# Batch 1's attention output as plain float32 products, the weight decode spread over steps, expert 0 loaded in stage 3, and later block gathers

## The chip, the cores and the metric

One core of one Trainium2 chip. The metric is the device time of the kernel in microseconds (us), the median of several executions. The engines are TensorE (PE, its weight loads PEld), VectorE (DVE), ScalarE (ACT), GpSimd (POOL) and SyncE (SP, which issues most of the DMAs). The instructions of one engine run in order.

## The reference

Three parts follow each other; all data are float32:

```python
# attention: 4 batches, 8 heads, 576 positions, 64 wide
decay = cum[:, :, :, None] - cum[:, :, None, :]      # cum = cumsum(log f)
attn  = softmax(where(causal, -1e9, q @ k.T / 8 + decay))
x     = (attn @ v) regrouped to 2304 tokens x 512
# MoE1, dense: 512 -> 1536 -> 512
x = (silu(x @ w_gate) * (x @ w_val)) @ w_out
# MoE2, top-1 of 8 experts, 512 -> 1024 -> 512
out[t] = gate_w[t] * eom[t, e] * (relu(x[t] @ w1[e]) @ w2[e]),  e = argmax(x[t] @ w_gate)
```

## The kernel before

**Number form.** Most products run in float32r. An operand is split into a high part (a copy to float32r, by ACT) and a low part (the difference, by DVE or POOL), and a product is the sum of two or three float32r products.

**Attention** (class Attention, L41 to L290) handles one head at a time. `load` (L96) brings q, k and v in; `split` (L105) makes high and low parts, those of v at L126 (ACT) and L127 (POOL); `qk` (L130) makes scores (L152, L153), their maximum (L156, DVE) and the exponential (L164, ACT). `tr` (L168) transposes the exponentials in four groups into PSUM and writes a high part `ath` (ACT, L191) and a low part `atl` (DVE, L192). `av` (L195) multiplies them by v: ten matmuls at L207 for positions 64 to 575 and two at L216 for the first 64. The stationary operand holds high v in 64 columns and low v in the other 64, so half of the result is moved by ACT (L211, L217) and added by DVE (L212, L218). `xout` (L238) normalises and splits the head pair into `xth` and `xtl`, the input of MoE1.

**MoE1** (class MoE1, L305 to L435) has five stages of 12 units, one stage for each token chunk of 512 or 384 (the last is reordered). A unit is `gv` (24 matmuls, L378, then tanh and two DVE operations) and, one unit later, `out` (12 matmuls, L403). Both are generators that yield after every three matmuls, 12 steps for a unit; at each step the loop in `tile_kernel` also runs a share of the attention of the next batch (`MIX`, L448). So heads 0 to 7 run alone, heads 8 to 15 (batch 1) during stage 0, and batches 2 and 3 during stages 1 and 2.

**Decode.** The MoE1 weights lie in memory as 64-bit words (`mw`). In stage 0 each of the 36 pieces is loaded (L328, one of two `raw` buffers), squared (L332, ACT), worked on by four DVE operations (L333 to L336), and split into the weight tile (L338, ACT; L339, POOL). A finished tile is also written back to DRAM (L341, L343, by SP), from which later stages fetch it (`fetch`, L345, by POOL's queue). `ready` (L353) emits the decode of the unit three ahead in one go, two pieces when a `gv` ends and one when an `out` ends; six pieces are emitted at the start of stage 0.

**MoE2** (class MoE2, from L660). Per expert, token rows are gathered (L709, POOL), transposed (L693), split (L695, L696); four units of `g1` (24 matmuls of 304 columns, L728) and `g2` (24, L743) follow. `load_expert` (L647) brings a quarter of one expert: two loads of 512 KB (L652), each split by ACT (L654) and DVE (L655) into two tiles of the weight pools. The quarter u=0 of expert 0 is loaded near the end of MoE1 (L1019, through the two buffers of the pool `raw2`), the quarters 1 to 3 after MoE1 (L1059). Tokens beyond the 304 slots of an expert go to a block: `block_a` (L780, called at expert 4, quarter 3) gathers rows and weights (`b_y`, `b_g`, `b_r`, all by L709), `block_b` (L833, called at expert 6) multiplies them.

**Order.** A scheduler orders each engine's instructions by priority, which is the order of the program text, and by its own estimate of readiness. `tc.issue_after(x)` keeps what it encloses behind x.

Of the kernel before, what the change touches and what calls it, by code (L numbers as in the profile page):

```python
# [40 lines left out]
class Attention:  # L41
    def __init__(self, tc, ctx, cst, io, xth, xtl, ps_s, ps_t, ps_x):
# [14 lines left out]
        fix = pool("at_fix", 1, side="right")  # L57
        self.e0 = [fix.tile([128, 128], F32, name=f"e0_{i}") for i in range(2)]
# [4 lines left out]
        for t in self.e0 + [t.bitcast(F32) for t in self.hl]:  # L63
            nc.gpsimd.memset(t, 0.0)
# [31 lines left out]
    def load(self, h):  # L96
        nc = self.nc
        qk = self.raw.tile([128, 2, S], F32, name="qkd")
        for o in (0, 64):
            nc.sync.dma_start(out=qk[o:o + 64], in_=self.io["qk"][h])  # L100
        v = self.raw.tile([128, 5, D], F32, name="vraw")
        nc.sync.dma_start(out=v, in_=self.io["vL"][h])
        self.R[h] = qk, v

    def split(self, h):  # L105
# [17 lines left out]
        self.K[h] = (a, b, kh, kl)  # L123
        vs = self.stk.tile([128, 5, 2, D], F32R, name="vs")
# [43 lines left out]
    def tr(self, h, g):  # L168
# [15 lines left out]
        else:  # L184
# [3 lines left out]
            nc.tensor.transpose(tp[:, 256:384], E[h, 0], ident)  # L188
        th = self.ap[g].tile([128, n], F32R, name=f"ath{g}")
# [5 lines left out]
    def av(self, h):  # L195
# [6 lines left out]
        z, c = self.Z[h // 2]  # L202
        ax = self.ps_x()
        terms = [(0, 0, 0, 512, 0), (1, 1, 0, 512, 0), (2, 2, 0, 384, 128), (4, 2, 384, 128, 384), (3, 3, 0, 256, 256)]
        for t, (j, g, s, n, d0) in enumerate(terms):
            for i in range(2):
                nc.tensor.matmul(ax[:, d0:d0 + n], st[:, j], self.T[h, g][i][:, s:s + n],  # L207
                                 start=t == 0 and i == 0, stop=t == 4 and i == 1)
            if t == 1:
                yield 900  # L210
        nc.scalar.activation(c[m:m + 64, 64:], ax[o:o + 64], ACTF.Copy)  # L211
        nc.vector.tensor_add(z[m:m + 64, 64:], ax[m:m + 64], c[m:m + 64, 64:])  # L212
        yield 600
        ay = self.ps_t()
        for i in range(2):
            nc.tensor.matmul(ay[:, :64], st[:, 0], self.T[h, 3][i][:, 256:320], start=i == 0, stop=i == 1)  # L216
        nc.scalar.activation(c[m:m + 64, :64], ay[o:o + 64, :64], ACTF.Copy)  # L217
        nc.vector.tensor_add(z[m:m + 64, :64], ay[m:m + 64, :64], c[m:m + 64, :64])  # L218
        for g in range(4):
            del self.T[h, g]  # L220
        yield 220
# [83 lines left out]
class MoE1:  # L305
    def __init__(self, tc, ctx, io, xth, xtl):
# [8 lines left out]
        self.dec = None  # L315

    def decode(self, ft, kind):
# [14 lines left out]
        nc.scalar.activation(s, hv.bitcast(F32), ACTF.Square)  # L332
        nc.vector.tensor_scalar(t, hv, 0x07ffffff, 3, op0=ALU.bitwise_and, op1=ALU.logical_shift_left)  # L333
        nc.vector.scalar_tensor_tensor(t, hv, -0x40000000, t, op0=ALU.bitwise_and, op1=ALU.bitwise_or)  # L334
        nc.vector.scalar_tensor_tensor(t, lv, 29, t, op0=ALU.logical_shift_right, op1=ALU.bitwise_or)  # L335
        nc.vector.scalar_tensor_tensor(s, s, 2.0 ** -30, t.bitcast(F32), op0=ALU.is_ge, op1=ALU.mult)  # L336
        s3 = s.rearrange("p (a b) -> p a b", a=4)
# [14 lines left out]

    def ready(self, i, out):  # L353
# [4 lines left out]
        elif out:  # L358
            self.decode(i, 2)
        else:  # L360
            self.decode(i, 0)
            self.decode(i, 1)
# [49 lines left out]
    def steps(self, done):  # L412
# [7 lines left out]
        for i in range(len(us) + LAG):  # L420
            if i < len(us):
                u = us[i]
                yield u
                yield from self.gv(u)
# [3 lines left out]
            if i >= LAG:  # L428
                u = us[i - LAG]
                yield from self.out(u)  # L430
# [16 lines left out]
APB = (1, 2, 1, 1)  # L447
MIX = 0.46  # L448
# [211 lines left out]
class MoE2:  # L660
# [47 lines left out]
    def gather(self, dst, src, ix):  # L708
        self.nc.gpsimd.indirect_dma_start(out=dst, out_offset=None, in_=src[:, :],  # L709
# [227 lines left out]
def tile_kernel(tc, io, out, dbg=None):  # L937
    nc = tc.nc
    with ExitStack() as ctx:
# [19 lines left out]
        with ExitStack() as cx:  # L959
# [5 lines left out]
            for i in range(3):  # L965
                m1.decode(0, i)
# [17 lines left out]
        slots, w00 = None, None  # L984
# [10 lines left out]
        for st in m1.steps(done):  # L995
            if isinstance(st, tuple):
                if st[0] != stage:
# [4 lines left out]
                    if stage == 0:  # L1002
                        for i in range(6):
                            m1.decode(1 + i // 3, i % 3)
# [5 lines left out]
                    if stage == 3:  # L1010
# [6 lines left out]
                        wts.pools = [pool(ctx, "wA", 6, side="right")]  # L1017
                        raw = pool(cm, "raw2", 2)
                if st[0] == 4 and st[2] == 4 * NF + 5:  # L1019
# [107 lines left out]
```

## Time and profile before

| | us |
|---|---|
| median of 3 runs (lowest, highest) | 1080.6 (1076.13, 1085.01) |
| the profiled execution | 1079.55 |
| its span in the trace | 1077.8 |
| heads 0 to 7 alone | 0 to 94 |
| stage 0 of MoE1, with batch 1's heads and 33 decodes | 94 to 296 |
| stages 1, 2, then 3 and 4 of MoE1 | 296 to 468, to 617, to 775 |
| routing tail | 775 to 796 |
| MoE2 | 796 to 1066 |

The trace is that of one execution. Times count from the start of the span. The busy time of an engine in a stretch says how much work it had; what a stage is bound by is read from the waits and from the chain of work that ended last. The end of a matmul is modelled, so its pace is read from the starts of long uninterrupted rows.

### The profile page before, as it was taken

The numbers are of one execution on the slowest core, as the hardware profiler recorded it, in microseconds if no ns is written. First come the engines' busy times: TensorE is split into PE (matmuls) and PEld (weight loads), VectorE is DVE, ScalarE is ACT, GpSimd is POOL, SyncE is SP. The second block draws the span as 40 slices with busy tenths as digits, with TensorE's granted clock in tenths as the row PEclk, the third lists the DMA queues.
The fourth block names the chain that finished last, engine by engine and source line by source line (L and its number), as shares of the span: only waits on it lengthen the run. The fifth ranks groups of instructions, "written<-read, shape, count | busy, mean of one in ns | idle before, by whom it ended". The sixth has DMA issues, their size and how long they took to land.

```text
span 1077.8 us, 15687 instructions
## 1 busy us (share of the span) xinstructions
PE 974.9 (90%) x5488; PEld 837.4 (78%) x5488; DVE 583.1 (54%) x1293; ACT 523.5 (49%) x1083; POOL 428.8 (40%) x463
## 2 busy tenths in 40 slices
PE   3788788888899999999999999999987999999894
PEld 2666566665667787777777899999876999999794
DVE  6779998888654644344444431152274555452820
ACT  5697555555465545465454431221233544543721
POOL 4556664455443443533442323223154633332111
PEclk9798999999989999999999999999978999999998
DMA  7646565657966565765444577367458656552500
GB/s 203 171 115 186 191 225 198 221 190 234 301 159 190 164 173 158 191 203 167 145 147 130 192 244 240 106 212 241 169 177 304 192 173 189 168 173 76 170 28 26
DMA packets 69956, 192.49 MB, mean 179 GB/s; under 512 B 9317, under 2 KB 29815, under 8 KB 62580
## 3 DMA queue, kind: packets, MB, share of 16 engines
q1 hardware_dynamic: 51411, 106.51, 33.1%
q0 software_dynamic: 18464, 84.96, 24.6%
q8 instruction: 44, 0.72, 0.3%
q14 instruction: 37, 0.29, 0.1%
HBM read 158.10 MB, written 29.14 MB: 174 GB/s over the span
## 4 chain that ended last, share of the span: by engine, by line
PE 50%; issue 15%; DVE 6%; POOL 5%; DMA 4%; ACT 2%; POOLq 0%; SPq 0%; DVEq 0%; ACTq 0%
PE ps_g L378 21%; PE ps_y L403 11%; PE ps_t L207 3%; PE m_psy L743 3%; PE m_psg L728 2%; POOL out L769 2%; PE ps_s L152 1%; DMA raw<-mw 1%; PE ps_s L153 1%; DMA raw<-w 1%; DVE dt L335 1%; DMA qb<-qkh 1%; POOL yg L709 1%; DVE dt L334 1%; PE ps_t L179 1%
## 5 line engine op out<-in xcount | busy, mean ns | idle before, releaser
L728 PE MATMUL m_psg<-ygh,w 128*128 128x304 f32 x512 | 117.3, 310 | 6.9 <-DVE h2l L731 4.2
L743 PE MATMUL m_psy<-h2h,w 128*128 128x304 f32 x512 | 115.7, 308 | 0.1
L192 DVE TENSOR_TENSOR atl<-ps_t,ath 128x512 fp32r<-128x512 f32 (+1 forms) x128 | 81.3, 636 | 51.6 <-ACT ath L191 51.4
L164 ACT ACTIVATE e<-e,mx 64x64 f32<-64x64 f32 (+4 forms) x160 | 88.9, 557 | 35.7 <-DVE mx L156 34.4
L655 DVE TENSOR_TENSOR w<-raw,w 128x1024 fp32r<-128x1024 f32 x64 | 77.2, 1229 | 50.2 <-ACT w L654 27.6
L191 ACT ACTIVATE ath<-ps_t 128x512 fp32r<-128x512 f32 (+1 forms) x128 | 70.3, 554 | 61.5 <-PE ps_t L183 18.0
L389 POOL TENSOR_TENSOR hl<-hs,hh 128x512 fp32r<-128x512 f32 (+1 forms) x60 | 70.9, 1181 | 60.7 <-ACT hh L388 60.6
L383 DVE SCALAR_TENSOR_TENSOR hs<-hs,ps_g 128x512 f32<-128x512 f32 (+1 forms) x60 | 37.9, 631 | 103.9 <-ACT hs L382 103.8
L728 PEld LDWEIGHTS m_psg<-ygh,w 128*128 128x128 f32 x512 | 87.1, 192 | 7.9 <-DVE h2l L731 4.4
L156 DVE CUSTOM_DVE_ANT_0 e<-ps_s,mask 64x64 f32<-64x64 f32 (+4 forms) x160 | 66.6, 424 | 48.9 <-PE ps_s L153 42.9
L654 ACT ACTIVATE w<-raw 128x1024 fp32r<-128x1024 f32 x64 | 67.4, 1058 | 46.2 <-DMA raw<-w 16.7
L743 PEld LDWEIGHTS m_psy<-h2h,w 128*128 128x128 f32 x512 | 86.7, 190 | 0.9 <-issue 0.5
L769 POOL DMA_INDIRECT out<-o,sl_idx x24 | 31.5, 1313 | 121.1 <-ACT o L765 120.2
L152 PE MATMUL ps_s<-qkh 128*128 128x288 f32 (+3 forms) x192 | 62.8, 338 | 18.4 <-DVE qkh L121 9.2
L743 PE MATMUL m_psy<-h2l,w 128*128 128x304 f32 x256 | 78.4, 306 | 1.2 <-issue 1.2
L728 PE MATMUL m_psg<-ygl,w 128*128 128x304 f32 x256 | 78.1, 305 | 0.0
L382 ACT ACTIVATE hs<-ps_g 128x512 f32<-128x512 f32 (+1 forms) x60 | 33.1, 551 | 87.8 <-PE ps_g L378 73.5
L731 DVE SCALAR_TENSOR_TENSOR h2l<-m_psg,h2h 128x304 fp32r<-128x304 f32 x64 | 30.2, 472 | 67.7 <-ACT h2h L730 66.4
L153 PE MATMUL ps_s<-kl,qb 68*128 68x288 f32 (+3 forms) x192 | 57.8, 317 | 8.3 <-DMA qb<-qkh 8.2
L121 POOL TENSOR_TENSOR qkh<-qkd,qkh 64x576 fp32r<-64x576 f32 x31 | 45.6, 1472 | 46.3 <-ACT qkh L118 41.6
L152 PEld LDWEIGHTS ps_s<-qkh 128*128 128x128 f32 (+1 forms) x192 | 36.1, 191 | 35.8 <-DVE mx L156 20.6
L388 ACT ACTIVATE hh<-hs 128x512 fp32r<-128x512 f32 (+1 forms) x60 | 35.1, 585 | 56.6 <-DVE hs L385 56.5
(934 smaller groups left out, 2756.3 us busy)
## 6 DMA issues: line engine op xcount, KB each, us to landing
raw<-w SPq DMA_DIRECT2D x64, 512.0 KB
qkd<-qk SPq DMA_DIRECT2D x64, 288.0 KB
raw<-mw SPq DMA_DIRECT2D x36, 512.0 KB
vraw<-vL SPq DMA_DIRECT2D x32, 160.0 KB
qb<-qkh SPq DMA_DIRECT2D x32, 144.0 KB
yd<-yr SPq DMA_DIRECT2D x18, 256.0 KB
wdg<-wg__284 SPq DMA_DIRECT2D x1, 1024.0 KB
wdg<-wg__1288 SPq DMA_DIRECT2D x1, 1024.0 KB
```

The costliest lines, as they stand in the source:

```text
L152: nc.tensor.matmul(ps[:m, :n], a[:, q0:w], kh[:, lo:hi], start=True, stop=False)
L153: nc.tensor.matmul(ps[:m, :n], b[:, q0:w], kl[:, lo:hi], start=False, stop=True)
L164: nc.scalar.activation(e[:m, :w], e[:m, :w], ACTF.Exp, bias=prev[:m], scale=-1.0, accum_out=rs[:m, c:c + 1])
L191: nc.scalar.activation(th, tp[:, :n], ACTF.Copy)
L192: nc.vector.tensor_sub(tl, tp[:, :n], th.bitcast(F32))
L378: nc.tensor.matmul(p, w[:, a, 4 * m + k], x, start=k == 0 and j == 0, stop=k == 3 and j == 2)
L389: nc.gpsimd.tensor_sub(hl, t, hh.bitcast(F32))
L403: nc.tensor.matmul(self.Y[c][d], w[:, a, d], x, start=first and j == 0, stop=last and j == 2)
L654: nc.scalar.activation(hi, r, ACTF.Copy)
L655: nc.vector.tensor_sub(lo, r, hi.bitcast(F32))
L728: nc.tensor.matmul(ps[:, :C], w[:, k, fs], x[:, k], start=(k == 0 and c == 0), stop=(k == 3 and c == 2))
L743: nc.tensor.matmul(self.P[e][d][:, :C], w[:, f, ds], h[:, f], start=(u == 0 and f == 0 and c == 0), stop=(u == 3 and f == 1 and c == 2))
```

## The change

The change has four parts, and a constant for each is set anew.

1. **Decode one operation at a time.** `decode` becomes a generator that yields after each of its first five operations. `ready` only queues pieces (`queue`); each step of MoE1 pulls one operation, or two if more than three pieces are queued; `flush` completes a piece before the unit that uses it.
2. **Batch 1 in plain float32** (`WIDE`, heads 8 to 15). The transposed exponentials are copied once, as float32 (groups 0 and 2 by ACT, 1 and 3 by DVE), the products of `av` are five and one instead of ten and two, with plain v in a stationary operand whose other 64 columns are zero, and ACT alone writes z. v is loaded straight into that operand (`load_v`, after the products of the head two before), so it needs no split. The shares of attention (`MIX`) and buffers of one group (`APB`) change with it.
3. **Expert 0 loaded early.** Three quarters are loaded around the end of stage 2, into a pool opened there; only the fourth is loaded after MoE1.
4. **Block gathers later.** `block_a` is placed behind the last gather emitted before it.

```diff
@@ class Attention
+        self.vst = [fix.tile([128, 5, 2, D], F32, name=f"vst{i}") for i in range(2)]
...
+    def load_v(self, h):
+        if WIDE[0] <= h < WIDE[1]:
+            self.nc.sync.dma_start(out=self.vst[h % 2][:, :, h % 2], in_=self.io["vL"][h])
+            self.V[h] = self.vst[h % 2]
...
+        if WIDE[0] <= h < WIDE[1]:
+            t = self.ap[g].tile([128, n], F32R, name=f"at{'hl'[h % 2]}{g}").bitcast(F32)
+            if g % 2:
+                nc.vector.tensor_copy(t, tp[:, :n])
+            else:
+                nc.scalar.activation(t, tp[:, :n], ACTF.Copy)
+            self.T[h, g] = (t,)
+            return
...
-            for i in range(2):
+            for i in range(parts):
...
+        if wide:
+            yield 1000
+            nc.scalar.activation(z[m:m + 64, 64:], ax[m:m + 64], ACTF.Copy)
+        else:
+            nc.scalar.activation(c[m:m + 64, 64:], ax[o:o + 64], ACTF.Copy)
+            nc.vector.tensor_add(z[m:m + 64, 64:], ax[m:m + 64], c[m:m + 64, 64:])
...
+        if h >= WIDE[0]:
+            self.load_v(h + 2)
@@ class MoE1
         nc.scalar.activation(s, hv.bitcast(F32), ACTF.Square)
+        yield
         nc.vector.tensor_scalar(t, hv, 0x07ffffff, 3, op0=ALU.bitwise_and, op1=ALU.logical_shift_left)
+        yield
...
+    def queue(self, ft, kinds):
+        self.dq += [(ft, k, self.decode(ft, k)) for k in kinds]
+
+    def pull(self):
+        if self.dq and next(self.dq[0][2], 0) == 0:
+            self.dq.pop(0)
...
-        elif out:
-            self.decode(i, 2)
         else:
-            self.decode(i, 0)
-            self.decode(i, 1)
+            self.queue(i, (2,) if out else (0, 1))
@@ constants
-APB = (1, 2, 1, 1)
-MIX = 0.46
+APB = (1, 1, 1, 1)
+MIX = (0.62, 0.46, 0.46)
+WIDE = (8, 16)
@@ tile_kernel
-                        wts.pools = [pool(ctx, "wA", 6, side="right")]
+                        wA, wC = pool(ctx, "wA", 6, side="right"), pool(ctx, "wC", 12, side="right")
+                        wts.pools = [wA, wC, wC]
...
-                if st[0] == 4 and st[2] == 4 * NF + 5:
-                    w00 = load_expert(nc, io, wts, raw, 0, 0)
+                if st[0] == 4 and st[2] >= 4 * NF + 3 and st[2] % 2:
+                    w00.append(load_expert(nc, io, wts, raw, 0, len(w00)))
...
+            for _ in range(2 if len(m1.dq) > 3 else 1):
+                m1.pull()
-            while att and ca_ < cm_ * MIX:
+            while att and ca_ < cm_ * MIX[stage]:
...
-                for u in range(1, 4):
+                for u in range(len(w00), 4):
...
-                    blk = m2.block_a(pblk, cur, rt)
+                    with tc.issue_after(m2.pmark.ins):
+                        blk = m2.block_a(pblk, cur, rt)
```

What moves on SP in stage 0, where `vraw` and `vst` are the buffers of v, `raw` those of the decode, `wdg` and `wdo` the write-backs. Before, some units into the stage:

```order
L100 DMA qkd<-qk 64x1152 [waits DMAHW4_49]
L328 DMA raw<-mw 128x1024 [waits DMAHW5_49,DVE_49,Activation_49]
L102 DMA vraw<-vL 128x320 [waits DMAHW6_49,Pool_49]
L114 DMA qb_156<-cd 2x576 [waits DMAHW7_49,PE_49]
L341 DMA wdg_83<-wg__1288 128x2048 [waits DMAHW0_49,Pool_49]
L328 DMA raw<-mw 128x1024 [waits DMAHW1_49,DMAHW3_49,DVE_49,Activation_49]
L343 DMA wdo_84<-wo__1312 128x1024 [waits DMAHW2_49,Pool_49]
```

And now, at the same place:

```order
L101 DMA qkd<-qk 64x1152 [waits DMAHW4_49]
L112 DMA vst_152<-vL 128x5x64 [waits DMAHW5_49,PE_49]
L359 DMA raw<-mw 128x1024 [waits DMAHW1_49,DVE_49,Activation_49]
L377 DMA wdg_85<-wg__1447 128x2048 [waits DMAHW7_49,Pool_49]
L379 DMA wdo_86<-wo__1505 128x1024 [waits DMAHW0_49,Pool_49]
L359 DMA raw<-mw 128x1024 [waits DMAHW2_49,DVE_49]
L359 DMA raw<-mw 128x1024 [waits DMAHW6_49,DVE_49,Activation_49]
```

The load of v now waits for PE (the products of the head two before) and has the next decode's load behind it; before, it waited for POOL.

On SP at the boundary of stages 2 and 3, from the last load of attention on; `raw<-w` are the loads of expert 0 and `yd<-yr` the rows that MoE1 writes for the gathers. Before:

```order
L119 DMA qb_158<-qkh 64x576 [waits DMAHW7_49,Activation_49]
L652 DMA raw<-w 128x4x256 [waits DMAHW3_49,DMAHW2_49,DMAHW5_49,DMAHW1_49,DMAHW6_49,DMAHW0_49,DMAHW7_49,PE_49,Activation_49]
L652 DMA raw<-w 128x2x512
L503 DMA yd<-yr 128x512 [waits Activation_49] x2
L503 DMA yd<-yr 128x512 [waits DMAHW4_49,Activation_49]
```

Now:

```order
L129 DMA qb_160<-qkh 64x576 [waits DMAHW7_49,Activation_49]
L699 DMA raw<-w 128x4x256 [waits DMAHW3_49,DMAHW2_49,DMAHW5_49,DMAHW1_49,DMAHW6_49,DMAHW0_49,DMAHW7_49,PE_49,Activation_49]
L699 DMA raw<-w 128x2x512
L699 DMA raw<-w 128x4x256 [waits DMAHW0_49,DVE_49,Activation_49]
L699 DMA raw<-w 128x2x512 [waits DMAHW1_49,DVE_49]
L699 DMA raw<-w 128x4x256 [waits DMAHW4_49,DMAHW2_49,DVE_49]
L699 DMA raw<-w 128x2x512 [waits DMAHW3_49,DVE_49]
L550 DMA yd<-yr 128x512 [waits Activation_49] x6
```

All six loads stand ahead of the row writes, and the third to sixth wait until ACT and DVE have emptied the two buffers. The conversions stand in ACT's queue between the operations of the units that run there.

On POOL at the start of MoE2, `yg` are gathers of token rows, `b_r` and `b_y` those of the block. Before:

```order
L709 DMA yg<-yd,sl_idx 48x512
L709 DMA b_r_9994<-w,b_wi 128x1024
L709 DMA yg<-yd,sl_idx 128x512 x2
L709 DMA yg<-yd,sl_idx 48x512
L709 DMA b_r_9998<-w,b_wi 128x1024
L709 DMA b_r_10002<-w,b_wi 128x1024
L709 DMA b_r_10006<-w,b_wi 128x1024
L709 DMA yg<-yd,sl_idx 128x512
```

Now:

```order
L756 DMA yg<-yd,sl_idx 48x512
L756 DMA yg<-yd,sl_idx 128x512 x2
L756 DMA yg<-yd,sl_idx 48x512
L756 DMA yg<-yd,sl_idx 128x512 x2
L756 DMA yg<-yd,sl_idx 48x512
L756 DMA gate<-gd,sl_idx 128x1 x2
```

The twelve gathers of `b_r` have left this place; they stand between the output scatters of a middle expert, behind the row gathers of expert 5.

## Rows read from the trace of the kernel before

**Rows 1.** Busy time of each engine in stretches of the span, core 0.

```profile
core 0: us, PE busy (x) PEld busy (x) DVE busy (x) ACT busy (x) POOL busy (x), PEclk, DMA share, GB/s
...
94.00:296.00 202.00, 165.24 (x754) 125.70 (x754) 171.99 (x298) 110.53 (x231) 107.96 (x94) 0.94 0.69 220
...
775.00:834.00 59.00, 44.20 (x251) 38.95 (x250) 33.83 (x100) 24.21 (x40) 25.24 (x24) 0.83 0.73 248
834.00:999.00 165.00, 164.56 (x1197) 162.12 (x1197) 82.50 (x114) 79.34 (x129) 62.76 (x55) 1.00 0.51 159
```

**Rows 2.** Groups of instructions on DVE in stage 0, 94 to 296 us.

```profile
line engine op names shapes xcount | busy us, mean ns | idle before us <-releasers
L335 DVE SCALAR_TENSOR_TENSOR dt<-raw,dt 128x512 int32<-128x512 int32 x33 | 33.8, 1023 | 0.1
L334 DVE SCALAR_TENSOR_TENSOR dt<-raw,dt 128x512 int32<-128x512 int32 x32 | 33.7, 1053 | 0.4
L336 DVE SCALAR_TENSOR_TENSOR ds<-ds,dt 128x512 f32<-128x512 f32 x33 | 27.8, 843 | 0.3
L333 DVE TENSOR_SCALAR dt<-raw 128x512 int32<-128x512 int32 x31 | 25.2, 814 | 3.2 <-DMA raw<-mw 3.2
L192 DVE TENSOR_TENSOR atl<-ps_t,ath 128x512 fp32r<-128x512 f32 (+1 forms) x32 | 20.3, 635 | 9.8 <-ACT ath L191 9.7
...
L212 DVE TENSOR_TENSOR z<-ps_t,c 64x512 f32<-64x512 f32 x7 | 4.8, 683 | 0.1
...
L218 DVE TENSOR_TENSOR z<-ps_t,c 64x64 f32<-64x64 f32 x8 | 1.7, 218 | 1.0 <-ACT c L217 0.9
```

**Rows 3.** SP's waits in stage 0, longest in total first.

```profile
engine line waited for: us in total, times, longest us
SPq L328 <- DVE dt L335: 57.4, 19, 5.1
SPq L341 <- POOL wg__1918 L339: 7.1, 1, 7.1
```

**Rows 4.** The chain that ended last, from 264 to 276 us in stage 0.

```profile
261.57 2.95 DVE dt L335
264.52 0.02 SPq L328
264.55 0.03 issue
264.57 8.35 DMA raw<-mw
272.92 0.02 issue
...
273.59 0.42 ACT ath L191
274.01 0.48 ACT hs L382
274.49 0.53 ACT wg__2737 L338
```

**Rows 5.** Groups on ACT in stage 0, 94 to 296 us.

```profile
L332 ACT ACTIVATE ds<-raw 128x512 f32<-128x512 f32 x32 | 21.4, 668 | 10.6 <-DMA raw<-mw 9.3 <-POOL wg__1325 L339 0.9 <-POOL wg__1563 L339 0.2
```

**Rows 6.** The chain from 648 us on, in stage 3, PE uninterrupted (384 columns).

```profile
648.49 4.16 PE ps_g L378 x24
652.65 2.08 PE ps_y L403 x12
```

**Rows 7.** The chain at the start of MoE2, 796 to 840 us.

```profile
799.55 5.05 DMA raw<-w
...
817.84 7.46 DMA raw<-w
...
828.41 0.42 PE m_pst L693 x4
...
833.84 3.34 PE m_psg L728 x24
```

**Rows 8.** Groups on PE at the start of MoE2, 796 to 834 us.

```profile
L728 PE MATMUL m_psg<-ygh,w 128*128 128x304 f32 x66 | 16.7, 329 | 5.2 <-DVE h2l L731 4.2 <-ACT ygh L695 0.6 <-issue 0.4
L743 PE MATMUL m_psy<-h2h,w 128*128 128x304 f32 x48 | 12.1, 334 | 0.1
L728 PE MATMUL m_psg<-ygl,w 128*128 128x304 f32 x33 | 10.7, 326 | 0.0
L743 PE MATMUL m_psy<-h2l,w 128*128 128x304 f32 x24 | 8.0, 333 | 1.2 <-issue 1.2
```

**Rows 9.** POOL's groups from 788 to 834 us.

```profile
L709 POOL DMA_INDIRECT b_r<-w,b_wi x12 | 13.0, 1080 | 3.7 <-issue 3.7
```

**Rows 10.** DMA share in two 27-us stretches (columns as in rows 1).

```profile
270.00:297.00 27.00, 21.73 (x104) 16.85 (x103) 16.70 (x37) 13.34 (x31) 11.47 (x14) 0.94 1.03 297
810.00:837.00 27.00, 19.65 (x114) 18.51 (x114) 12.95 (x17) 10.73 (x15) 10.83 (x11) 0.87 0.82 285
```

**Rows 11.** Loads of expert weights in SP's time line, start and length.

```profile
598.97 0.95 SPq L652 DMA_DIRECT2D raw<-w  x2
770.57 2.25 SPq L652 DMA_DIRECT2D raw<-w  x4
798.41 29.68 SPq L652 DMA_DIRECT2D raw<-w  x12
```

**Rows 12.** ACT's conversions: near the end of stage 2, and early in MoE2.

```profile
605.48 1.06 ACT L654 ACTIVATE w<-raw 128x1024 fp32r<-128x1024 f32 x1 [2.14 <-DMA raw<-w]
...
796.08 2.00 ACT L654 ACTIVATE w<-raw 128x1024 fp32r<-128x1024 f32 x2
...
811.68 1.06 ACT L654 ACTIVATE w<-raw 128x1024 fp32r<-128x1024 f32 x1 [3.77 <-DMA raw<-w]
...
818.28 1.06 ACT L654 ACTIVATE w<-raw 128x1024 fp32r<-128x1024 f32 x1 [1.72 <-DMA raw<-w]
```

## Prediction made before the changed kernel ran

> **What bounds the kernel now.** I read the stretches first, then the waits and the chain inside the two stretches that lose time, and last the groups, for prices. In the stretches PE is busy nearly all the time from stage 1 on, but not in two places [rows 1]. In stage 0 it is busy 165.2 of 202 us, with DVE busiest at 172.0. Around the start of MoE2 it is busy 44.2 of 59 us. Only there can this change win much; later MoE2 (164.6 of 165 us) has nothing to give.
>
> Stage 0: the groups on DVE show that decoding takes 33.8 + 33.7 + 27.8 + 25.2 = 120.5 us of the 172, and batch 1's attention 20.3 us for the low parts and 6.5 us for the adds into z [rows 2]. SP's waits show the other limit: the next load of a piece waited 19 times, 57.4 us together, for L335, which frees one of the two buffers [rows 3]. The chain shows both in a row: DVE's L335 ends, SP issues, the load takes 8.35 us, and ACT, whose queue stands behind the square of that piece, then runs the transposed copy, tanh and weight copy that PE needs [rows 4]. How fast the pipeline could be at that load time: a buffer is taken for 8.35 us of loading, 0.67 us of the square [rows 5] and 0.81 + 1.05 + 1.02 us of DVE [rows 2], 11.9 us; with two buffers, 33 pieces need 33 x 11.9 / 2 = 196 us. A shorter load helps, but at the end of the stage the DMA share is 1.03 at 297 GB/s, the highest I see [rows 10]. So stage 0 is held by two things of nearly the same size, DVE's work and the buffers.
>
> Start of MoE2: from 796 to 834 us PE runs 66 + 33 + 48 + 24 = 171 matmuls [rows 8]. Uninterrupted, 24 take 3.34 us, 0.139 each, and four transposes 0.42 us [rows 7]. So 171 x 0.139 + 12 x 0.105 = 25.0 us of work took 38 us: 13.0 us are lost. The chain says to what: weight loads of 5.05 and 7.46 us [rows 7], for which ACT's conversions wait, 3.77 and 1.72 us among others [rows 12]. SP issued twelve of them between 798 and 828 us [rows 11], and in the same time POOL issued twelve gathers of block weights [rows 9], at 285 GB/s [rows 10].
>
> **The change, part by part.**
>
> *Batch 1 in float32, engines beside PE.* Per head DVE loses four subtractions (635 ns) and both adds (683 and 218 ns), and gets two copies. A copy of that shape does not stand in the rows; between nothing and the price of the subtraction I take the latter, since both read the same PSUM tile. That saves 2 x 0.635 + 0.901 = 2.17 us a head, 17.4 us for eight heads, and 27 at the other end [rows 2]. ACT and POOL lose work too (two of four copies, the split of v), but neither is the bound.
>
> *Batch 1 in float32, PE.* Columns per head: 512 + 512 + 384 + 128 + 256 + 64 = 1856, before twice. At 24 matmuls of 384 columns in 4.16 us [rows 6], a pass costs 1856 x 0.451 ns = 0.84 us, before 1.68. A plain float32 product does not occur in this trace. If it took one pass, PE would gain 6.7 us over eight heads; at the pace of the float32 transposes, 0.105 us for 128 columns [rows 7], it takes 14.5 x 0.105 = 1.52 us, and PE gains 1.3. Each pass more costs 6.7 us. PE is free 37 of 202 us [rows 1], so I take 0 for the stage, and keep both sides.
>
> The Trainium skill speaks against that ("FP8 and Floating Point Precision", section "TensorE Precision Notes"): true float32 makes four passes through the array. No run shows it yet. By that page the products take 3.35 us a head, 13.4 us more than before over eight heads, and the sum would be 1074 us if none of it were hidden.
>
> *Decode one operation at a time.* No operation is removed; 6 pulls a piece, 12 steps a unit, two pulls while more than three pieces wait, so three pieces a unit can be done. DVE's decode operations now stand between others instead of in a burst, so attention's scores and tanh wait less; the piece keeps its buffer for more steps, which costs when buffers are the bound. Bounds: nothing, or the 37 us that PE is free, either way. A square that waits for its load still stops ACT's queue as in [rows 4].
>
> *Stage 0 together.* If DVE is the bound, stage 0 follows its work: -17 us, -27 at most. If the buffers are, the stage stays near 196 us, -6. I take -12, the middle; it can also lose, because the load of v now waits for PE on SP with raw loads behind it, six times (heads 10 to 15). Range -28 to +12. One buffer less for a transposed group costs nothing that I see: the product that reads it stands ahead of the next write.
>
> *Expert 0 early.* Six of the twelve loads and conversions of 796 to 828 us leave that place. The fourth quarter and expert 1's first are loaded from 770 us on, as four loads were before [rows 11]. What stays is that about three conversions of 1.0 us stand in ACT's queue ahead of the first operation of the first unit [rows 12]. So the 13.0 us shrink to about 3: -10, between -5 and -12.
>
> Where they go: the boundary of stages 2 and 3, where before two loads were issued at 598.97 us [rows 11] and ACT waited 2.14 us for the first [rows 12]. From issue to conversion went 6.5 us. Now two more pairs follow through the same two buffers, each issued only when the pair before is converted, and ACT's queue with tanh and copies of the units stands behind each. A unit there is 4.16 + 2.08 = 6.24 us of PE [rows 6], about one load, so PE mostly has work. I take +2, one wait like the one shown; 0 if all is hidden, +8 if both pairs stop ACT for 4 us more than the shown wait's cover.
>
> *Block gathers later.* Their traffic leaves 796 to 834 us (counted above). Later MoE2 moves 159 GB/s [rows 1], well under the 297 seen, so the 138 GB/s between carry the 4 MB (twelve gathers of 128 rows, four of 1024 floats and eight of 512) in some 30 us. The loads there are four buffers ahead. I take +1, from 0 to +5: loads of 7.46 instead of 5.05 us [rows 7] would use up the lead.
>
> **Sum.** The profiled execution took 1079.55 us, 1.05 below the median of the runs. 1079.55 - 12 - 10 + 2 + 1 = 1060.5 us.
>
> **Rivals.**
>
> *A, the buffers hold stage 0.* DVE gets freer, but two buffers, loads of 8 us and the share of 1.03 stay, and the spread decode keeps a buffer longer. For it: [rows 3, 4]. Against it: 57 of 202 us waited is not all, and DVE's own queue lengthens L335. Stage 0 at -1: 1079.55 - 1 - 10 + 3 = 1071.5 us.
>
> *B, DVE was all of it.* Its 17 to 27 us of work go, the bursts no longer hold up scores, and stage 0 runs at 177 us. For it: DVE's share of 85% [rows 1]. -25: 1047.5 us.
>
> *C, slower: SP is held by PE.* The load of v waits for the products of the head two before, which with the larger attention share come late, and the raw loads behind it, then the write-backs, wait along; ACT stops at the square, PE at the weights. For it: SP waits already reach 7.1 us [rows 3]. At about 6 us for each of six loads stage 0 is 36 us later, and with DVE's relief of 12 to 14 about +23: 1079.55 + 23 - 7 = 1095.5 us. It decides from 3 us a load on, as less is covered by the wait for the buffer (57.4 / 19 = 3.0 us, [rows 3]).
>
> *D, the early loads cost what they save.* ACT waits at the boundary (+8), later gathers take +5: 1079.55 - 12 - 10 + 13 = 1070.5 us.
>
> *E, dear products.* Two passes more than before cost 13.4 us of PE; the heads' chain of transposes, products and z is longer by as much, and nothing hides it: 1060.5 + 13.4 = 1073.9 us. Against it stand PE's 37 free us. The four passes of the Trainium skill, cited above, would be this case.
>
> **Chances and range.** Forecast (about 1053 to 1068) 0.40, A 0.20, B 0.17, C 0.10, D 0.08, E 0.05. One per cent, 10.8 us, is about what a measurement tells from no change: faster means under 1069.8, slower over 1091.4. Forecast and B are faster, so are a quarter of A and half of D: 0.66. C is slower, 0.10, and 0.24 remain. The range of 1040 to 1084 us leaves out C and the far half of B.
>
> **What would show it.** Right: stage 0 of about 190 us, DVE busy near 155 us there, SP's wait for the buffers (now behind L369) well below 57 us; MoE2's first 171 matmuls in about 28 us; no ACT wait over 3 us around 600 to 625 us. The price of a float32 product stands in the starts of five matmuls of one head. Wrong: SP waiting for PE before a load of v (C), a wait for the buffers as long as before (A), PE idle after 605 us (D), or a PE work in stage 0 over 175 us (E).

## The result, and the profile after

The changed kernel takes 1093.0 us (median of 4 runs, 1092.1 to 1094.1), before 1079.3; the ratio is 1.0118 with an interval of 1.0092 to 1.0144. It is 1.2% slower, clear of the noise. The profiled execution took 1092.09 us, its span is 1090.3.

Where the 12.5 us of span come from is read from the starts of PE's matmuls, 24 of `gv` or `g1` for a unit, in both traces:

| point | before | after | gained or lost up to here since the row above |
|---|---|---|---|
| first unit of stage 0 | 94.1 | 99.1 | +5.0 |
| second unit of stage 1 | 312.6 | 322.2 | +4.6 |
| first unit of stage 3 | 611.3 | 619.0 | -1.9 |
| third unit of stage 3 | 627.5 | 642.9 | +7.7 |
| first unit of MoE2 | 796.2 | 811.0 | -0.6 |
| unit 4 of MoE2 | 833.7 | 836.3 | -12.2 |
| unit 16 of MoE2 | 923.5 | 925.7 | -0.4 |
| unit 18 of MoE2 | 938.2 | 952.1 | +11.7 |
| end of the span | 1077.8 | 1090.3 | -1.4 |

The stretches that answer to [rows 1] (same columns): DVE has 14 us less to do in stage 0, PE 5 us more, and the stage is not shorter. At the start of MoE2 PE runs without a break; but there are two new gaps, in 624 to 640 us (11.7 of 16 us busy) and in 850 to 1010 us, where before PE lost nothing.

```profile
99.00:300.00 201.00, 170.78 (x753) 124.53 (x752) 157.75 (x276) 103.07 (x217) 101.06 (x84) 0.94 0.66 211
...
624.00:640.00 16.00, 11.69 (x46) 9.25 (x45) 7.96 (x10) 8.82 (x15) 1.97 (x4) 0.79 0.69 228
...
811.50:850.00 38.50, 38.50 (x279) 38.04 (x279) 21.73 (x31) 18.15 (x29) 14.84 (x14) 1.00 0.62 194
850.00:1010.00 160.00, 151.25 (x1078) 148.43 (x1077) 72.77 (x103) 71.90 (x118) 67.00 (x59) 0.97 0.55 178
```

DVE's groups in stage 0 answer to [rows 2]. The decode costs the same, the sixteen copies of L204 stand for the 32 subtractions, at 590 and 586 ns each; so the saving is there as priced.

```profile
L367 DVE SCALAR_TENSOR_TENSOR dt<-raw,dt 128x512 int32<-128x512 int32 x32 | 34.3, 1072 | 0.6
L369 DVE SCALAR_TENSOR_TENSOR dt<-raw,dt 128x512 int32<-128x512 int32 x32 | 33.1, 1033 | 0.4
...
L204 DVE COPY ath<-ps_t 128x512 f32<-128x512 f32 (+1 forms) x8 | 4.7, 590 | 12.3 <-PE ps_t L191 8.4 <-PE ps_t L200 3.9
L204 DVE COPY atl<-ps_t 128x512 f32<-128x512 f32 (+1 forms) x8 | 4.7, 586 | 2.4 <-PE ps_t L200 1.4 <-PE ps_t L191 1.0
```

SP's waits in stage 0 answer to [rows 3]: the buffers are waited for as long as before, and the new load of v waits for PE only 3.2 and 0.5 us.

```profile
SPq L359 <- DVE dt L369: 59.2, 15, 8.5
...
SPq L112 <- PE ps_s L165: 3.2, 1, 3.2
...
SPq L112 <- PE ps_t L242: 0.5, 1, 0.5
```

Four of the losses, each from the chain that ended last (start, length, what). First, before stage 0: POOL runs `kl` of the next head (L132) ahead of the second half of the normalisation (L262), for which PE and the last piece of MoE1's input wait. In the kernel before, POOL had done both halves by 92.6 us.

```profile
93.72 0.54 POOL hl L261
94.26 1.35 POOL kl L132
95.61 0.62 POOL hl L262
96.23 0.04 issue
96.28 0.47 PE ps_t L264
```

Second, the end of stage 0: SP issues the transfer of the next head's q, high part (L129), only behind two write-backs of decoded weights, and the second waits for POOL's subtraction of the last piece. The transfer then takes 8.47 us, and PE waits 6.7 us for it.

```profile
300.28 1.31 POOL wo__2956 L375
...
301.61 0.34 SPq L379
...
302.00 8.47 DMA qb<-qkh
310.47 0.14 issue
310.61 0.61 PE ps_s L165
```

The kernel before has the same order at this place, but there PE had other work and waited 2.0 us:

```profile
285.17 0.33 SPq L343
...
286.21 8.05 DMA qb<-qkh
```

Third, the boundary of stages 2 and 3: the second and third pair of early loads take 5.67 and 6.54 us each, ACT stands at their conversions, and the copy of MoE1's rows (L549) and with it PE (L547) wait behind.

```profile
617.68 5.67 DMA raw<-w
...
623.37 1.07 ACT w L701
...
624.46 1.24 DVE w L702
...
625.72 6.54 DMA raw<-w
...
632.28 1.06 ACT w L701
633.33 0.49 ACT yr L549
```

PE's only waits from 600 to 645 us are these; there is none for a fetched weight:

```profile
PE ps_r L547 <- ACT yr L549: 3.1, 1, 3.1
PE ps_r L547 <- ACT yc L540: 1.1, 3, 0.7
```

Fourth, the gathers of block weights, now at 929.6 to 950 us. The chain there names no engine:

```profile
925.85 2.89 PE m_psg L775 x12
...
929.22 0.47 DVE h2l L778
929.70 6.18 another core or an unknown queue
935.88 0.02 issue
935.90 0.47 DVE y2t L798
936.38 0.38 DVE h2l L778
936.76 4.81 another core or an unknown queue
941.57 0.02 issue
941.59 0.48 DVE y2t L798
```

DVE's copy of the products waits only for PE. PE's matmul records run on at 0.14 us up to 932.4 us, yet PE's semaphore told of their ends at 933.0, 935.9, 939.4 and 941.6 us, while nearly everywhere else the two agree within 0.02 us. DVE's copies started at 935.90 and 941.59 us, right after these times. So PE had not finished them when the records say.

A fifth loss lies in the first six units of stage 0 (92.3 us before, 103.8 now, in part because they hold a larger share of attention). PE waits there for the normalisation's product on DVE (L276), which stands in DVE's queue behind decode operations (L365 to L371), here four of them:

```profile
143.33 0.98 DVE dt L365
...
144.34 3.03 DVE dt L367
...
147.39 1.64 DVE dt L369
...
149.13 0.69 DVE ds L371
149.82 0.61 DVE z L276
...
150.47 0.30 PE ps_t L279
```

PE's waits from 99 to 325 us show it as the longest group:

```profile
PE ps_t L279 <- DVE z L276: 9.2, 3, 4.4
PE ps_s L165 <- DMA qb<-qkh: 6.7, 1, 6.7
```

The same wait (L248 for L245) took 2.8 us in the kernel before.

### The profile page after: what moved, and what is told of

Same layout as the page of the kernel before. It is cut to its first block, busy times and chain, and to the rows that moved or that the text cites. A ratio compares the mean times of both kernels' runs of the same rounds, so it can differ in the third digit from the quotient of the medians.

```text
span 1090.3 us, 15632 instructions
## 1 busy us (share of the span) xinstructions
PE 982.9 (90%) x5488; PEld 840.0 (77%) x5488; DVE 569.8 (52%) x1261; ACT 512.7 (47%) x1059; POOL 425.9 (39%) x457
## 3 DMA queue, kind: packets, MB, share of 16 engines
q0 software_dynamic: 18464, 84.96, 24.2%
## 4 chain that ended last, share of the span: by engine, by line
PE 59%; issue 13%; DVE 11%; DMA 6%; POOL 5%; ACT 4%; another core or an unknown queue 1%; SPq 1%; POOLq 0%; ACTq 0%; DVEq 0%
PE ps_g L422 23%; PE ps_y L447 10%; PE m_psg L775 6%; PE m_psy L790 5%; PE ps_t L229 3%; DVE dt L367 2%; DVE ds L371 2%; DVE dt L369 2%; PE ps_s L164 2%; PE ps_s L165 2%; POOL out L816 1%; DMA qb<-qkh 1%; DVE dt L365 1%; DMA raw<-mw 1%; DMA raw<-w 1%
## 5 line engine op out<-in xcount | busy, mean ns | idle before, releaser
L433 POOL TENSOR_TENSOR hl<-hs,hh 128x512 fp32r<-128x512 f32 (+1 forms) x60 | 73.5, 1224 | 65.0 <-ACT hh L432 65.0
L701 ACT ACTIVATE w<-raw 128x1024 fp32r<-128x1024 f32 x64 | 67.5, 1060 | 41.3 <-PE m_psg L775 16.4
L212 DVE TENSOR_TENSOR atl<-ps_t,ath 128x512 fp32r<-128x512 f32 x96 | 61.1, 638 | 44.2 <-ACT ath L211 43.9
L164 PE MATMUL ps_s<-qkh 128*128 128x288 f32 (+3 forms) x192 | 64.1, 344 | 16.2 <-DVE qkh L131 9.3
L211 ACT ACTIVATE ath<-ps_t 128x512 fp32r<-128x512 f32 x96 | 52.6, 554 | 43.6 <-PE ps_t L200 13.4
```

Of the source, the lines that this page charges most:

```text
L164: nc.tensor.matmul(ps[:m, :n], a[:, q0:w], kh[:, lo:hi], start=True, stop=False)
L212: nc.vector.tensor_sub(tl, tp[:, :n], th.bitcast(F32))
L433: nc.gpsimd.tensor_sub(hl, t, hh.bitcast(F32))
L701: nc.scalar.activation(hi, r, ACTF.Copy)
```

## The experiments

All figures of this table are from the starts of PE's matmuls in each kernel's trace, and from runs beside the kernel before on the same chip. The letter of a label names a group of runs on one chip: e on chip 14, f on 7, g on 15, h and i on 13; for before and after the chip is not on record. The row of the kernel before and its trace are of that first chip; its median beside e, f, g, h and i was 1076.7, 1079.7, 1081.8, 1075.9 and 1076.9 us. "Stage 0" goes from its first unit to the second of stage 1, "boundary" over two units (16.2 us undisturbed), "start" over units 0 to 4 of MoE2, "gathers" over units 16 to 18.

| kernel | begins | stage 0 | boundary | start | gathers | median us | ratio to before |
|---|---|---|---|---|---|---|---|
| before | 94.1 | 218.5 | 16.2 | 37.4 | 14.8 | 1079.3 | |
| after | 99.1 | 223.1 | 23.9 | 25.3 | 26.4 | 1093.0 | 1.0118 |
| e1_eager | 95.3 | 213.6 | 22.6 | 25.3 | 14.8 | 1064.5 | 0.9890 |
| e2_split | 93.1 | 213.8 | 22.7 | 25.8 | 14.8 | 1069.3 | 0.9946 |
| e3_oneload | 100.7 | 220.7 | 16.2 | 26.0 | 14.8 | 1077.0 | 1.0011 |
| e4_blkearly | 99.5 | 222.8 | 21.0 | 30.1 | 14.8 | 1083.5 | 1.0072 |
| f1_gspread | 98.9 | 222.0 | 24.0 | 25.3 | 15.3 | 1086.6 | 1.0059 |
| f2_place | 99.4 | 222.7 | 16.2 | 25.6 | 27.1 | 1088.2 | 1.0086 |
| f3_wbpool | 97.1 | 218.7 | 21.8 | 25.3 | 26.6 | 1094.1 | 1.0145 |
| f4_best | 95.8 | 211.2 | 16.2 | 25.3 | 15.4 | 1063.1 | 0.9832 |
| g1_again | 100.2 | 223.6 | 22.1 | 25.6 | 26.6 | 1096.8 | 1.0162 |
| g2_mix46 | 100.2 | 223.9 | 23.8 | 25.3 | 26.0 | 1096.9 | 1.0150 |
| g3_onepull | 100.8 | 208.7 | 24.8 | 25.3 | 25.9 | 1079.5 | 0.9992 |
| g4_pulllast | 95.7 | 214.3 | 24.2 | 25.7 | 26.1 | 1083.0 | 1.0028 |
| h1_last | 98.6 | 214.8 | 16.2 | 25.3 | 14.8 | 1064.0 | 0.9881 |
| h2_eager | 94.0 | 212.2 | 21.8 | 25.7 | 14.8 | 1065.4 | 0.9904 |
| h3_split | 99.6 | 218.4 | 16.2 | 25.8 | 14.8 | 1067.5 | 0.9910 |
| i1_after | 101.0 | 223.7 | 24.0 | 25.4 | 14.8 | 1082.4 | 1.0046 |
| i2_eager | 95.7 | 213.9 | 23.8 | 25.3 | 14.8 | 1067.8 | 0.9913 |

**One part undone at a time.** `e1_eager` drains the generator where a piece is queued:

```diff
-        self.dq += [(ft, k, self.decode(ft, k)) for k in kinds]
+        for k in kinds:
+            for _ in self.decode(ft, k):
+                pass
```

> The changed kernel with the decode in bursts again (all operations of a piece at once, where it is queued); all else as changed. Theory S1, the spread decode is what made stage 0 late (last piece done at 297.8 us against 282.0 before, gaps of up to 4 us between a freed buffer and the next load): the first unit of stage 1 starts about 10 us earlier than in the changed kernel (300.2), total about 1085 us. Rival S2, the plain float32 products and the larger attention share did it: first unit of stage 1 stays within 3 us of 300, total 1093 us.

`e2_split` sets `WIDE` past the last head, with shares and buffers of before (`WIDE = (99, 99)`, `MIX` 0.46, `APB = (1, 2, 1, 1)`, no fixed tiles for v):

> The changed kernel with batch 1 in high and low parts again (attention shares and buffers as before); the spread decode, early loads and later gathers stay. S1 (spread decode is what costs): stage 0 as late as in the changed kernel or later, since DVE gets 17 us of work back; total 1093 to 1105 us. S2 (float32 products cost): first unit of stage 1 at about 290 us, total about 1083 us.

`e3_oneload` loads one quarter early (`if st[0] == 4 and st[2] == 4 * NF + 5`):

> The changed kernel with only the first quarter of expert 0 loaded early, the other three after MoE1 as before; gathers stay late. Theory L1, six early loads through two buffers stop ACT at the boundary of stages 2 and 3 (7.5 us there in the changed kernel), and the start of MoE2 was slow before because of the gathers of block weights, not of the loads: the boundary wins 7 us back, the start loses 3 us at most; total about 1088 us. Rival L2, the loads held the start: boundary -7, start +10 us; total about 1096 us.

`e4_blkearly` calls `block_a` without `issue_after`:

> The changed kernel with the block's gathers where they were before (free to run at the start of MoE2); early loads stay. Theory G1, a dense row of gathers of block weights stops PE for about 9 us wherever it stands: the stop at 928 to 942 us is gone, and one of 5 to 10 us stands at the start of MoE2; total 1088 to 1094 us. Rival G2, it is the place (middle of an expert, with the loads of its weights) that costs: the stop is gone and the start stays fast; total about 1083 us.

Both theories on stage 0 are half right. With either the bursts or the split heads stage 0 takes 214 us, 5 less than before; spread decode and float32 heads together, as the change has them, take 221 to 224. So neither part is slow by itself. The loads are the clearest: with one early load the boundary is back at 16.2 us and the start of MoE2 still takes 26.0 instead of 37.4 us (L1). So the loads alone do not hold that start. With all three early and the gathers back it takes 30.1, and what ended last there was still a load, of 15.67 us beside the row of gathers (`e4_blkearly`):

```profile
814.96 15.67 DMA raw<-w
```

The loads of [rows 7] took 5.05 and 7.46 us, so by this chain the gathers cost by holding up a load. Either move alone wins most of the 12 us (11.4 without the gathers, 7.3 with the early loads), but the 37.4 is from another chip. In none of these four kernels did PE stop at the gathers, though three have them in the same place; neither G1 nor G2 foresaw that.

**The losses mended one by one.** `f1_gspread` issues one item of the block's gathers behind each output scatter of experts 1 to 3; `f2_place` ties the conversions to the unit before them; `f3_wbpool` issues the write-backs from POOL:

```diff
+                    if items:
+                        with tc.issue_after(m2.pmark.ins):
+                            items.pop(0)()
...
-                    w00.append(load_expert(nc, io, wts, raw, 0, len(w00)))
+                    with tc.issue_after(m1.mk[0].ins), tc.issue_after(m1.mk[1].ins):
+                        w00.append(load_expert(nc, io, wts, raw, 0, len(w00)))
...
-            nc.sync.dma_start(out=self.wd[ft][0],
+            nc.gpsimd.dma_start(out=self.wd[ft][0],
```

> The changed kernel with the block's gathers spread, one item (512 KB) behind each output scatter of the experts 1 to 3, instead of twelve in a row. Theory G1 (a dense row of gathers stops PE when it stands in a bad phase): the stop of 11.6 us between units 16 and 18 of MoE2 is gone, the start stays fast, total 1081 us. Rival G3 (the stop at 928 us has nothing to do with the gathers): it stays, total 1093 us.

> The changed kernel with the six early conversions held in ACT's and DVE's queues behind the unit at which the program emits them (three units of the last stage), their loads unchanged. Theory L1 (ACT stood behind loads that had not landed): the boundary of stages 2 and 3 takes 16 us again instead of 24, nothing is lost elsewhere; total 7 to 8 us under the changed kernel, 1085 us. Rival L3 (the loads themselves crowd the fetches there): boundary as slow as in the changed kernel, 1093 us.

> The changed kernel with the write-backs of decoded weights issued by POOL, right behind its own subtraction, instead of by SP. Theory S3 (the raw loads wait on SP behind write-backs that wait for POOL, 3 to 7 us each, and that makes the spread decode late): the last piece of the decode ends 8 us or more earlier than 297.8, total about 1083 us. Rival S4 (order of the loads on SP is not what counts): within 3 us of 1093.

`f4_best` has the bursts of `e1_eager`, `f1_gspread` and `f2_place` together:

> Decode in bursts, batch 1 in float32, early loads with their conversions held in place, gathers spread: what the theories S (burst decode with float32 heads), L1 and G1 take for the best version. From the run with bursts (1064.5 us) less 6 us at the boundary of stages 2 and 3: 1058 us. If L1 is wrong, 1064 us.

`f2_place` takes the whole boundary loss away (23.9 to 16.2 us); the longest group of ACT's waits in the changed kernel from 600 to 645 us (below) is gone with it. But it does not leave the loads unchanged, as was expected: its conversions run from 741.9 us on, and since there are two buffers, the third to sixth load are issued from 744.3 to 757.9 us instead of 617.7 to 628.0. So this run alone does not tell L1 from L3. Against L3 stands that in the changed kernel PE waited there for ACT's copies only, 3.1 and 1.1 us, and for no fetch.

```profile
ACT w L701 <- DMA raw<-w: 9.6, 3, 4.5
```

`f1_gspread` leaves 0.5 of the 11.6 us, on a chip on which `f2_place` and `f3_wbpool` had all of it: without the row of gathers PE does not stop there. `f3_wbpool` is a miss with a lesson. DVE's last decode operation ends at 268 us instead of 300, and the loss at the end of stage 0 is gone (the first unit of stage 1 takes 12.6 instead of 22.0 us), so SP's order did cost that; but the first six units take 113.1 instead of 103.8 us, and late pieces are thereby not the cause of stage 0's slow first half. `f4_best` is the fastest kernel of all, 0.9832 (0.9795 to 0.9869), 5 us over what was expected; it lost 5 us between units 4 and 12 of MoE2 in a stop of the same kind with no gather of block weights near it. A row of gathers stands there all the same: from 813.0 to 825.2 us POOL issues nine of `gate`, 128x1 each, with 0.3 us between them, and the stretch moves 88 GB/s:

```profile
818.00:823.00 5.00, 2.99 (x21) 2.51 (x19) 1.05 (x3) 1.45 (x3) 3.78 (x5) 1.00 0.25 88
```

**Why the two parts do not go together.** `g1_again` is the changed kernel; `g2_mix46` has `MIX = (0.46, 0.46, 0.46)`; `g3_onepull` pulls once a step; `g4_pulllast` has the pulls behind the attention's share:

```diff
-            for _ in range(2 if len(m1.dq) > 3 else 1):
-                m1.pull()
             while att and ca_ < cm_ * MIX[stage]:
...
+            for _ in range(2 if len(m1.dq) > 3 else 1):
+                m1.pull()
             cr_ += 1
```

> The changed kernel once more, beside the three below. Theory G4 (the stop of PE at the gathers of block weights hangs on the run and the chip, not on the kernel's parts): units 16 to 18 of MoE2 take either 15 or 26 us, and the other kernels of this call, whose gathers stand at the same place, take the same. Rival G5 (it hangs on what the changed kernel does before): 26 us here whatever the others show. Total 1083 us without the stop, 1093 us with it.

> The changed kernel with the share of attention in stage 0 at 0.46 instead of 0.62. Theory A1 (spread decode and float32 heads each win about 5 us up to the second unit of stage 1 and lose 5 together because the larger share runs the heads ahead of the decode): up to that unit 8 us are won against g1_again. Rival A2 (the bunching of decode operations in DVE's queue, which the share doesn't cure): no more than 3 us, or a loss.

> The changed kernel with one decode operation a step always (what is missing is completed in a row ahead of its unit). Theory A3 (two pulls a step bunch the decode and hold up the heads): 5 us or more are won up to the second unit of stage 1. Rival A4 (the decode is then late, in rows of up to 14 operations): 5 us or more lost.

> The changed kernel with the decode operations emitted behind the step's share of attention instead of ahead of it. Theory A2 (decode operations ahead of score maxima and normalisation on DVE: ACT's exponentials waited 23 us for maxima in stage 0, 6 to 17 us in the kernels that are fast there): 8 us are won up to the second unit of stage 1, that wait falls under 15 us. Rival A1: within 3 us of g1_again there.

One pull a step wins 14.9 us in stage 0 (A3), the pulls behind the attention 9.3, and 4.5 ahead of it; the smaller share wins nothing, it moves the loss (unit 6 is 14 us earlier, the first unit of stage 1 takes 34.8 us). So A1 falls. A2's time came, its sign did not: ACT waited 21.0 us for maxima in `g4_pulllast`, 22.5 in `g1_again`. Both winners change the order of few instructions. The first unit of stage 1 takes 12.6 and 12.7 us instead of 21.5, because the transfer of q no longer stands behind the last write-back (it is issued at 294.5 and 295.6 us, not at 304.2), and that is what the loss at the end of the stage came from. The rest follows PE's wait for the normalisation, which A2 named beside the maxima. In the first six units it takes 8.2 us in all seven traces that leave this part of the change as it is (102.4 to 105.0 us for these units), 5.4 with the pulls behind the attention (100.7), and nothing with one pull a step (94.4) or with bursts (95.7 to 97.7); `f3_wbpool`, with 2.6 us of it, loses its time there elsewhere. From 99 to 325 us in `g3_onepull`:

```profile
PE ps_t L279 <- DVE z L276: 0.9, 2, 0.7
```

How late stage 0 begins needs care. From POOL's first normalisation step (L228 before, L259 now) to the first unit it takes 5.5 us in the kernel before, 10.2 in all ten kernels with the changed order, 8.7 in `g4_pulllast` and `h1_last`, and 5.6 to 6.2 with bursts. When that step itself starts varies from 86.9 to 91.0 us, also between kernels with the same order on POOL there (87.0 and 89.9 us in `g4_pulllast` and `h1_last`), and no part of the change explains that. So of the 4.5 us ahead of stage 0 in `g4_pulllast` its order accounts for 1.6.

**Do the repairs add up, and whose is the stop.** `h1_last` is `g4_pulllast` with `f1_gspread` and `f2_place`; `h2_eager` and `i2_eager` are `e1_eager` again; `h3_split` is `h1_last` with the split heads of `e2_split`; `i1_after` is the changed kernel.

> The changed kernel with three of its four late places mended: decode operations emitted behind the attention share, early conversions held in place, gathers spread. If the losses are separate (13.8 us up to the second unit of stage 1, 7.6 us at the boundary of stages 2 and 3, 11 us at the gathers where the stop occurs), they add: 32 us under the changed kernel where the stop occurs, 21 us where it does not; about 1063 us, as the version with bursts (1063.1). If they hang together, 5 us or more are missing.

> The kernel with the decode in bursts once more, gathers in a row late as in the changed kernel. Its first run showed no stop of PE, nor did any kernel of that call; the next two calls showed it in all kernels with the gathers in a row. Theory G4 (chip or run): where h1_last or h3_split show events of that kind, this one shows the stop of 11 us between units 16 and 18 and takes about 1076 us; where they show none, it is at 1064. Rival G6 (bursts avoid it): 15 us between these units and no more than 1066 us.

> As h1_last, but batch 1 in high and low parts again. Tells what the float32 heads are worth once the late places are mended. Theory W1 (they cost about 6 us of PE and order in stage 0 and give about as much back where stage 1 begins): within 4 us of h1_last. Rival W2 (DVE's 17 us are won): 8 us or more slower than h1_last.

> The changed kernel unchanged, beside its version with the decode in bursts. Theory G4 (the stop of PE at the gathers in a row belongs to the chip): either both kernels of this call stop for about 11 us between units 16 and 18 of MoE2 (then about 1096 and 1076 us), or neither does (then about 1082 and 1064 us). Rival G6 (bursts avoid it): only this one stops.

> The version with the decode in bursts, gathers in a row late as in the changed kernel. G4: stops exactly when the changed kernel beside it does (1076 us then, 1064 us otherwise). G6: never stops, 1064 us while the changed kernel takes 1096.

`h1_last` is 27.8 us of span under the changed kernel's own profile: 8.8 to the second unit of stage 1, 7.7 at the boundary, 11.6 at the gathers. The last is not its merit, for on its chip the row of gathers does not stop PE (`h2_eager`). Against `i1_after` on the same chip it wins 19.9 us of span, 11.3 to the second unit of stage 1 and 7.8 at the boundary; 21 were expected where there is no stop, so the losses add up. `h3_split` is 3.4 us slower than `h1_last`, hardly more than the noise, so W1: the float32 heads are worth little. And the changed kernel itself has run with the stop (after, `g1_again`) and without it (`i1_after`: 1.0046 instead of 1.0162), on different chips. In the same stretch it shows PE busy for 18.0 of 18.0 us with the same gathers, and from 948 to 953 us still so at 393 GB/s (`i1_after`):

```profile
928.00:946.00 18.00, 18.00 (x132) 17.84 (x131) 10.49 (x13) 8.32 (x14) 14.04 (x14) 1.00 0.82 280
```

and in the first profile of the changed kernel:

```profile
925.00:943.00 18.00, 9.25 (x62) 8.49 (x60) 5.10 (x7) 3.59 (x6) 11.39 (x12) 0.82 0.71 253
```

In each group all kernels with the row of gathers at that place stopped, or none did. The kernel before fits: it takes 1075.9 to 1076.9 us beside the groups without the stop and 1079.3 to 1081.8 beside those with it. So G4 stands; whether the bursts would escape the stop (G6) stays open, since with the row late they never ran on a chip that had it.

## Why the prediction was wrong

**Stage 0, forecast -12, measured +4.6, and +5.0 ahead of it.** This term failed, and with it the sign: of the 31.6 us between the sum and the profiled execution 21.6 lie here. Two steps failed. The first is that the stage "follows its work" or the buffers, with the spread decode put at nothing because attention's scores would "wait less". DVE's work fell as worked out (172.0 to 157.8 us), but PE waited for single instructions in the wrong place of an in-order queue. It waited 9.2 us for the normalisation behind decode operations (2.8 before) and 6.7 us for the transfer of q (2.0 before). With the same operations pulled one a step (`g3_onepull`) the stage takes 208.7 us, 9.8 less than before: the relief was there, and the order ate it. The second is the price of the float32 products, put at 0 (next paragraph): PE was busy 180.0 of 218.5 us before, 186.0 of 223.1 now, and 184.9 of 208.7 in `g3_onepull`.

The 5 us ahead of the stage were in no term. The chain shows POOL's `kl` between the halves of the normalisation, and the stretch from L259 to the first unit took 10.2 us in every kernel with that order, 5.5 before. That it is `kl` is argued from the chain and was not tried alone. The order of the changed kernel shows these places; the prediction looked at it only at the load of v, for which SP waited 3.7 us in all.

**The price of a float32 product** was left between one pass and 1.8. Five products of one head, 1792 columns, stand in ten records:

```profile
257.16 3.17 PE ps_t L229 x10
```

That is 1.77 ns a column against 0.451 [rows 6], 3.9 passes. That agrees with the Trainium skill's four ("FP8 and Floating Point Precision", "TensorE Precision Notes"); the rows of the transposes were no upper bound. The case E that I gave 0.05 is part of what happened: PE had 5.5 us more to do in stage 0, and the float32 heads are worth 3.4 us in all, though DVE lost the 17 us of work.

**Start of MoE2, forecast -10, measured -12.2.** Right in size, half wrong in cause. I gave it to the early loads and let the gathers' move count along; `e3_oneload` shows that without the row of gathers one early load is enough (26.0 us), the other two are worth 0.7 us there. With the row in place (`e4_blkearly`) the early loads leave 30.1 us.

**Boundary, forecast +2 with an end at +8, measured +7.7.** The mechanism was named (ACT's queue behind loads through two buffers), the size taken from one wait although two more pairs were to come, whose loads took 5.7 and 6.5 us. PE waited 4.2 us for ACT's copies; the rest of the 7.7 fits its granted clock, which was 0.50 (1.2 GHz) from 634 to 638 us and 0.71 from 638 to 641 us, after the wait of 3.1 us, where the undisturbed kernel has 1.00.

**Late gathers, forecast +1 with an end at +5, measured +11.7** on chips with the stop, 0 on others. The free bandwidth was there, as the calm runs show. The rows from which I worked held the stop too: at the start of MoE2, PE's semaphore and its records disagree in the kernel before between 805 and 814 us, by up to 2.5 us, and I put that time down to loads.

**The rivals.** D named two of the losses, at the sizes +8 and +5. C reached the measured time from another wait, which is luck. A's sign came too, the wait for the buffers stayed at 59.2 us (57.4 before), but it does not decide: in `g4_pulllast` it is 67.5 us (96 to 297 us), and stage 0 is 9.3 us shorter than in `g1_again`. Without the stop the kernel before and the changed one differ by 0.5%, and its 1082.4 us lie inside my range; that would have been luck as well, for what was won at the start of MoE2 is given back in the queues at the other places.

## What to carry to other kernels

Removing work from the busiest engine of a stage buys time only if the order of every in-order queue still brings its neighbours their next instruction; compare the orders at the edges of a stage (the last write-back, the first load, the normalisation) before believing the sum. A load moved earlier moves its conversion too: hold the conversion in the queue at the place where it is due, or it stops the engine at the landing. Holding the conversions here held back the loads behind them too, as there were two buffers. Two changes that each win can lose together, so run each alone before keeping both, here the decode in bursts with the float32 heads (0.9832 with the conversions held and the gathers spread). Then ask whether it is their order that loses: one pull a step with the float32 heads has the shortest stage 0 of all (208.7 us), and with the other repairs it was not run.

## What the runs showed that I had not expected

PE can stop for 11 us with nothing to wait for: in a row of gathers of block weights it did so on some chips and not on others, with the same kernel. The sign is in no view of waits but in PE's semaphore against its matmul records (0.02 us apart as a rule, up to 9 us there) and in the granted clock, which fell to 0.5 (1.2 GHz) from 936.7 us on, after PE had gone idle. The block weights are not needed for it. In the ten traces of the first pair, f and g, the semaphore is over 0.3 us late, save in the last 20 us of the span, only in or within 4 us behind rows of indirect DMAs that POOL issues with 0.3 us between them: by up to 9.4 us at the long row, and by up to 3 us at a row of nine `gate` gathers near units 4 to 6. In the nine traces of chips 13 and 14, which have such rows too, it never is. What holds PE there is not settled: the loads, the gathers and POOL's issues were at the same offsets in runs without the stop.
